# Chunked attention with a gated MLP: a list of moves behind the planner reorders two stretches of the late products

## The chip, the cores and the metric

The kernel runs on one core of a Trainium2 chip. The metric is the device time of one launch in microseconds (us). Three runs of the kernel before took 373.38, 374.20 and 375.71 us, median 374.2.

The engines are PE (TensorE, matrix products; PEld is its weight load), DVE (VectorE), ACT (ScalarE), POOL (GpSimd) and SP (SyncE, which here only issues transfers).

## The reference

The reference computes a chunked attention and feeds its result into a gated MLP whose gate mixes positions:

```python
x = attn_out.transpose(0, 2, 1, 3).reshape(B, S, H * D)   # B=4, S=768, 512 wide
h = np.maximum(x @ w_in, 0.0)                             # 512 -> 1024
u, v = h[..., :512], h[..., 512:]
v_n = (v - mean(v)) / np.sqrt(var(v) + 1e-06)
v_s = np.einsum('ts,bsd->btd', w_spatial, v_n) + b_spatial[None, :, None]
out = (u * v_s) @ w_out
```

Every chunk of 32 positions attends to itself, 16 positions to its left, 8 to its right and 8 memory slots.

## The kernel before

The first part, up to about 218 us, interleaves the attention with the product with w_in. Its results, u and the normalized v, are written to scratch in device memory (`u_far`, `vn_far`) and read back later (`ug`, `vr`).

The second part is the subject here. For each of the four batches b there are two products: the spatial one (`spatial(b)`, v_n with w_spatial) and the w_out one (`ffn_o(b)`). Each is written as seven smaller products p1 to p7 of half-size blocks (`product`, seven in place of eight), whose left operands are quarters of the input or sums of quarters. In fp32 accuracy each operand is split in a high and a low half, and three matmuls replace one: high·high, low·high, high·low.

A small product goes through the engines in this way:

- `total` (L670, DVE, 128x768): sums or differences of quarters, s1 to s4, in `sm` tiles.
- `left` (L684 on ACT casts the high half, L687 on DVE subtracts for the low half, 128x768): the split operand in an `op` tile.
- `blocks` (L707, PE): 9 matmuls of 128x384 a block for the spatial product, two blocks a small product; 6 matmuls of 128x256 a block for w_out, three blocks a small product. The first matmul of a block reads the high half only, the second reads the low half.
- `done`: an accumulator in a `y` bank of PSUM runs on from small product to small product. Before p6 may add to the bank that p1 filled, ACT copies p1's value out (`take`, L747 for spatial, L812 for w_out). DVE adds results of PSUM (`join`, L753 and L818), adds the bias (L772) and multiplies u by the gate for one quarter (L791). POOL adds a bias step (L767) and multiplies the other quarters (L761).

Beside the first spatial product, two splits of w_out run too (`right_hand` and `split`): sums on POOL (L919), casts on ACT (L890), low halves on DVE (L894). The last pieces of the first part overlap it as well: the norm of the last v tile (L597, DVE, between a `pow` on POOL, L593, and a store to `vn_far`), and four blocks of u, whose relu on ACT (L619) writes a `uo` tile that a store takes to `u_far`. There are two `uo` buffers, so a relu waits until the store of the relu two before it has landed.

All operations are recorded in a list with an engine, an estimated duration, dependences and a rank (`Plan.op`). `Plan.order` simulates them with these estimates and gives one order for the whole program; `emit` issues them in that order. Each engine executes its own in that order and waits on semaphores; SP issues the transfers (L284) in that order too, each as soon as its own wait is over, so that a store whose data are late holds up all transfers behind it. Negative numbers in the order are idle matmuls at the start that keep PE busy.

Of the kernel before, what the change touches and what calls it, by code (L numbers as in the profile page):

```python
# [18 lines left out]
CH = 32  # L19
SLOT = 40  # L20
LEFT = 16
FIRST = ('a', 'b', 'w0', 'v0', 'w1', 'w2', 'w3', 'q1', 'v1', 'w4', 'v2', 'w5', 'w6', 'w7')
RANKS = (34.7, 9.5, 12.7, 26.3, 36.3, 2.9, 37.5, 38.2)
LOWS = ('POOL', 'DVE', 'DVE', 'DVE', 'POOL', 'DVE', 'DVE', 'POOL')
# [4 lines left out]
class Plan:  # L29
# [121 lines left out]
        return none  # L151

    def emit(self):
        for n in self.order():
            if n < 0:
                self.idle(-n)
            else:
                self.ops[n][2]()


@with_exitstack
def tile_chunked_attention_gmlp(
# [106 lines left out]
    def src(t, offset, ap):  # L269
        return bass.AP(tensor=t.tensor, offset=offset, ap=ap)  # L270
# [20 lines left out]
    def load(dst, src_, w, rank, r=(), eng="SP", slow=1.0, us=0.45, seq=False, drag=1.0, of=None):  # L291
        e = {"SP": nc.sync, "ACT": nc.scalar, "POOL": nc.gpsimd}[eng]
        n = 4
        for s in src_.shape:
            n *= s
        mb = n / 1e6 * slow
        n = op(eng, us, lambda: transfer(e, dst() if callable(dst) else dst, src_, mb, of), r=r, w=w, rank=rank, mb=mb,
               after=line.get(eng) if seq else None, drag=drag)
        if seq:
            line[eng] = n  # L300
# [10 lines left out]
    def spot(name, g, shape):  # L311
        if (name, g) not in t_:
            alloc(name, g, shape, F32)
        return t_[name, g]

    def load_qk(g, units=(0, 1), seq=True):
# [3 lines left out]
        nk = 2 * UT + CH  # L320
        lo = LEFT if c0 == 0 else 0
        hi = nk - LEFT if c0 + 2 * UC == NC else nk
        q0, q1 = units[0] * UT, units[-1] * UT + UT
# [5 lines left out]
        load(lambda: spot("k", g, [P, T, nk])[:, :, k0:k1],  # L329
             src(k, off - LEFT + k0, [[S, P], [P * S, T], [1, k1 - k0]]), w=[ks + (u,)], rank=10.0 * i, slow=1.15, seq=seq)  # L330

# [55 lines left out]
    def spread_mem(i, eng, rank):  # L387
        b, o = i // UB, (i % NV) * UC
        for r in range(2):
            rows = slice(r * D + CH, r * D + SLOT)  # L390

            def spread(rows=rows, r=r):
                to, of = vmain[rows, :, o:o + UC], memv[rows, b].unsqueeze(2).broadcast_to([M, T, UC, D])
                ins = {"DVE": nc.vector, "POOL": nc.gpsimd}[eng].tensor_copy(to, of)  # L394
                made.setdefault(("vmem", i % NV), []).append(ins.ins.name)
            op(eng, 1.1 if eng == "POOL" else 1.25, spread, r=[("memv", r)], w=[("vmem", i % NV, r)], rank=rank)
# [65 lines left out]
    def softmax(i, rank):  # L462
        c0 = (i % UB) * UC

        def top():
            s = t_["sx", i][:, :, 0]
            if c0 == 0:
                nc.vector.memset(s[0:CH, :, :, 0:LEFT], NEG)
            if c0 + UC == NC:
# [497 lines left out]
    for j in range(NV):  # L967
        spread_mem(j, "DVE" if j < 1 else "POOL", 1.0 + 10 * j)
    for x in FIRST:
        if x[0] == "w":  # L970
# [105 lines left out]
```

## Time and profile before

| quantity | value |
|---|---|
| runs, median (lowest to highest) | 374.2 us (373.38 to 375.71) |
| time of the profiled execution | 373.39 us |
| span of its trace | 371.6 us |
| PE busy | 356.2 us, 96% of the span |
| DVE, ACT, POOL busy | 294.7, 186.9, 157.1 us |
| granted PE clock | 1.00 of full speed |

The span runs from the program's first instruction to its last; 1.8 us of the profiled time lie around it. A busy PE says that matmuls are in flight. The two stretches of the change lie, in the trace of before, at about 206 to 262 us and at about 328 to 372 us.

### The profile page before, as it was taken

How to read it: one execution, taken by the hardware profiler on the slowest of the kernel's cores; microseconds unless marked ns; L12 is line 12 of the kernel's file. 1: busy time of each engine (PE TensorE's matmuls, PEld its weight loads, DVE VectorE, ACT ScalarE, POOL GpSimd, SP SyncE). 2: the span in 40 equal slices, each digit the busy share in tenths (PEclk: the TensorE clock that was granted, in tenths of full speed). 3: DMA queues.
4: the chain of work that ended last, by engine and by line, in shares of the span. 5: the costliest groups of instructions: out<-in, count | busy, mean ns of one | idle time of the engine just before them, and what ended most of it. 6: DMA issues, size and time to landing. Idle time of an engine off the chain costs nothing. (4 is left out here: it accounts for less than half of the span.)

```text
span 371.6 us, 11928 instructions
## 1 busy us (share of the span) xinstructions
PE 356.2 (96%) x5026; PEld 328.6 (88%) x5026; DVE 294.7 (79%) x480; ACT 186.9 (50%) x334; POOL 157.1 (42%) x154
## 2 busy tenths in 40 slices
PE   2899999999999999999999999999999999999995
PEld 2787888988889889889888899989999999999895
DVE  3799968669669499584797689999979896998894
ACT  3577553655555445544483445347434733744451
POOL 6254733366376057720024367851246025216400
PEclk9999999999999999999999999999999999999999
DMA  8998977885895894968743538204830572230015
GB/s 209 291 246 242 233 223 244 260 249 164 251 241 179 217 276 136 266 159 272 222 168 101 215 132 308 94 1 155 228 129 2 196 227 88 85 130 0 0 44 170
DMA packets 47557, 65.52 MB, mean 176 GB/s; under 512 B 4496, under 2 KB 38928, under 8 KB 47504
## 3 DMA queue, kind: packets, MB, share of 16 engines
q1 hardware_dynamic: 46848, 64.44, 58.1%
q8 instruction: 39, 0.64, 0.8%
q10 hardware_dynamic: 656, 0.33, 0.3%
q14 instruction: 14, 0.11, 0.1%
HBM read 45.88 MB, written 18.87 MB: 174 GB/s over the span
## 5 line engine op out<-in xcount | busy, mean ns | idle before, releaser
L707 PE MATMUL y<-wsp,op 128*128 128x384 f32 x288 | 52.4, 337 | 0.0
L761 POOL TENSOR_TENSOR ug<-st,ug 128x384 f32<-128x384 f32 x24 | 34.5, 1453 | 40.1 <-DVE st L753 35.6
L707 PEld LDWEIGHTS y<-wsp,op 128*128 128x128 f32 x288 | 49.9, 188 | 0.4 <-ACT st L747 0.3
L557 PE MATMUL f<-x,win_h 128*128 128x384 f32 x128 | 46.0, 359 | 0.2 <-issue 0.2
L559 PE MATMUL f<-x,win_h 128*128 128x384 f32 x128 | 43.2, 338 | 0.0
L558 PE MATMUL f<-x,win_l 128*128 128x384 f32 x128 | 43.2, 337 | 0.0
L557 PE MATMUL f<-win_h,x 128*128 128x512 f32 x96 | 41.1, 428 | 0.0
L707 PE MATMUL f<-wsp,op 128*128 128x384 f32 x216 | 39.7, 337 | 0.0
L687 DVE TENSOR_TENSOR op<-sm,op 128x768 fp32r<-128x768 f32 x32 | 36.6, 1144 | 2.0 <-ACT op L684 1.8
L558 PE MATMUL f<-win_h,x 128*128 128x512 f32 x96 | 37.9, 395 | 0.1
L707 PEld LDWEIGHTS f<-wsp,op 128*128 128x128 f32 x216 | 37.5, 188 | 0.3 <-DVE st L753 0.3
L559 PE MATMUL f<-win_l,x 128*128 128x512 f32 x96 | 37.7, 393 | 0.0
L707 PE MATMUL y<-wout,op 128*128 128x256 f32 x288 | 36.0, 281 | 0.9 <-DVE op L687 0.8
L455 DVE TENSOR_TENSOR xs<-sx,rec 128x512 f32<-128x512 f32 x24 | 16.6, 690 | 24.6 <-PE sx L415 24.4
L707 PEld LDWEIGHTS y<-wout,op 128*128 128x128 f32 x288 | 34.6, 188 | 1.6 <-DVE op L687 1.5
L593 POOL TENSOR_TENSOR rstd<-ve,mhalf 128x1 f32<-128x1 f32 x24 | 14.5, 604 | 49.0 <-DVE ve L589 47.1
L684 ACT CAST op<-sm 128x768 fp32r<-128x768 f32 x32 | 26.4, 836 | 16.5 <-DVE sm L670 16.4
L767 POOL TENSOR_TENSOR st<-st,bias 128x384 f32<-128x384 f32 x14 | 17.9, 1286 | 38.3 <-ACT st L747 28.7
L415 PEld LDWEIGHTS sx<-kmain,q 64*32 64x32 f32 x1536 | 17.3, 109 | 14.3 <-issue 12.9
L581 ACT ACTIVATE st<-f 128x512 f32<-128x512 f32 x24 | 14.4, 599 | 28.7 <-PE f L559 28.2
L415 PE MATMUL sx<-kmain,q 64*32 64x64 f32 x1536 | 21.3, 230 | 7.4 <-ACT kmain L400 6.8
L394 POOL COPY vmain<-memv 8x1024 f32<-8x1024 f32 x22 | 23.9, 1090 | 9.9 <-PE sx L415 7.7
(86 smaller groups left out, 780.9 us busy)
## 6 DMA issues: line engine op xcount, KB each, us to landing
vmain<-in_v_dram SPq DMA_DIRECT2D x48, 128.0 KB
u_far<-uo SPq DMA_DIRECT2D x32, 192.0 KB
vn_far<-st SPq DMA_DIRECT2D x24, 256.0 KB
vr<-vn_far SPq DMA_DIRECT2D x8, 768.0 KB
ug<-u_far SPq DMA_DIRECT2D x16, 384.0 KB
q<-in_q_dram SPq DMA_DIRECT2D x11, 512.0 KB
vmain<-in_v_dram SPq DMA_DIRECT2D x47, 96.0 KB
out_dram<-ot SPq DMA_DIRECT2D x33, 128.0 KB
```

The lines of the kernel that those rows point to most:

```text
L394: ins = {"DVE": nc.vector, "POOL": nc.gpsimd}[eng].tensor_copy(to, of)
L415: ins = nc.tensor.matmul(o, w_, m, start=True, stop=True, skip_group_check=True)
L455: nc.vector.tensor_tensor(xs.rearrange("p t r d -> p r t d"), t_["sx", i][:, :, 1], rec.rearrange("p t r -> p r t").unsqueeze(3).broadcast ...
L557: nc.tensor.matmul(o, lh, rh, start=(j == 0), stop=False)
L558: nc.tensor.matmul(o, ll, rh, start=False, stop=False)
L559: nc.tensor.matmul(o, lh, rl, start=False, stop=(j == len(pairs) - 1))
L593: nc.gpsimd.tensor_tensor(a, t_["ve", i], mhalf, op=ALU.pow)
L684: nc.scalar.copy(half(0), of())
L687: nc.vector.tensor_tensor(half(1), of(), half(0).bitcast(F32), op=ALU.subtract)
L707: nc.tensor.matmul(o, x, y, start=first and m == 1, stop=m == 3 * chunks, skip_group_check=True)
L761: nc.gpsimd.tensor_tensor(g, t_[st(x)], g, op=ALU.mult)
L767: {"DVE": nc.vector, "POOL": nc.gpsimd}[eng].tensor_tensor(a, a, bias[:, 1], op=ALU.add)
```

## The change

A table `MOVES` of 119 pairs is added. `emit` takes the planner's order, and for each pair (n, m) takes operation n out and puts it right behind operation m. The idle matmuls of the start are now a second table, and stand where they stood. Two lines of the table:

```diff
+MOVES = (
+    (1035, 934), (1027, 975), (1036, 941), (1028, 948), (1037, 1028), (1038, 1037), (963, 951), (964, 950),
...
+    (1507, 1506), (1479, 1507), (1509, 1479), (1502, 1498), (1523, 1502), (1499, 1505),
+)
+IDLES = ((87, 5), (92, 4), (95, 2), (104, 29), (132, 1))
...
     def emit(self):
-        for n in self.order():
-            if n < 0:
-                self.idle(-n)
-            else:
-                self.ops[n][2]()
+        order = [n for n in self.order() if n >= 0]
+        for n, m in MOVES:
+            order.remove(n)
+            order.insert(order.index(m) + 1, n)
+        idles = dict(IDLES)
+        for n in order:
+            self.ops[n][2]()
+            if n in idles:
+                self.idle(idles[n])
```

No operation is added, removed or resized. The planner's order has 1560 operations; the two stretches that change are places 961 to 1190 and 1422 to 1514 in it. Lines of the changed kernel stand 22 further down (L597 becomes L619).

The first place is DVE at the end of the first part, where the last v tile is normalized. `sm` tiles are the sums s1, s2 of the first spatial product, `op` tiles its split operands, `st_3848` (now `st_3850`) the last v tile. Before:

```order
L597 TENSOR_SCALAR st_3824<-st_3824,mvar_3831,rstd_3841 128x512
L585 BN_STATS stats_3857<-st_3848 128x6
L587 BN_AGGR mvar_3859<-stats_3857 128x2
L589 TENSOR_TENSOR ve_3861<-mvar_3859,eps_103 128x1
L687 TENSOR_TENSOR op_3855<-vr_3798,op_3855 128x768
L597 TENSOR_SCALAR st_3848<-st_3848,mvar_3859,rstd_3874 128x512
L670 TENSOR_TENSOR sm_3888<-vr_3798,vr_3809 128x768
L687 TENSOR_TENSOR op_3883<-vr_3809,op_3883 128x768
L670 TENSOR_TENSOR sm_3908<-sm_3888,vr_3798 128x768
L687 TENSOR_TENSOR op_3917<-sm_3908,op_3917 128x768
L670 TENSOR_TENSOR sm_3908<-vr_3809,sm_3908 128x768
L687 TENSOR_TENSOR op_3928<-sm_3888,op_3928 128x768
```

And with the change:

```order
L619 TENSOR_SCALAR st_3824<-st_3824,mvar_3831,rstd_3841 128x512
L692 TENSOR_TENSOR sm_3848<-vr_3798,vr_3809 128x768
L607 BN_STATS stats_3861<-st_3850 128x6
L609 BN_AGGR mvar_3863<-stats_3861 128x2
L611 TENSOR_TENSOR ve_3865<-mvar_3863,eps_103 128x1
L692 TENSOR_TENSOR sm_3867<-sm_3848,vr_3798 128x768
L709 TENSOR_TENSOR op_3859<-vr_3809,op_3859 128x768
L709 TENSOR_TENSOR op_3876<-sm_3867,op_3876 128x768
L709 TENSOR_TENSOR op_3857<-vr_3798,op_3857 128x768
L709 TENSOR_TENSOR op_3915<-sm_3848,op_3915 128x768
L619 TENSOR_SCALAR st_3850<-st_3850,mvar_3863,rstd_3888 128x512
```

Two sums and three more low halves now stand ahead of the last norm, which had only one low half between it and its statistics.

The second place is ACT right after that. `uo` tiles are the last relus of u, `y_3935` and `y_3969` (now `y_3950` and `y_3971`) the two banks that p1 fills; their copies into `st` tiles are the takes that p6 waits for. Before:

```order
L619 ACTIVATE uo_3922<-f_3894 128x384
L684 CAST op_3928<-sm_3888 128x768
L619 ACTIVATE uo_3945<-f_3913 128x384
L890 CAST wout_3958<-big_3358 128x256
L890 CAST wout_3958<-big_3373 128x2x256
L890 CAST wout_3958<-big_3459 128x256
L890 CAST wout_3958<-big_3495 128x2x256
L747 COPY st_3988<-y_3935 128x384
L684 CAST op_4002<-sm_3986 128x768
L747 COPY st_4009<-y_3969 128x384
```

And with the change:

```order
L641 ACTIVATE uo_3923<-f_3880 128x384
L912 CAST wout_3943<-big_3358 128x256
L912 CAST wout_3943<-big_3373 128x2x256
L641 ACTIVATE uo_3946<-f_3905 128x384
L641 ACTIVATE uo_3960<-f_3884 128x384
L769 COPY st_3986<-y_3950 128x384
L706 CAST op_3990<-sm_3984 128x768
L912 CAST wout_3943<-big_3459 128x256
L769 COPY st_4011<-y_3971 128x384
```

The last relu now stands right ahead of the first take, and one cast has moved in between the two takes. On PE, p6 now starts with the bank `y_3971`, whose take is the second of the two.

The third place is DVE at the end of the last spatial product. `ug_5127` is the quarter that DVE gates itself, `op_5355` (now `op_5346`) the operand of p1 of the last w_out product, `op_5359` (now `op_5348`) that of p2 of the w_out product before it, which PE runs right behind p1. Before:

```order
L791 TENSOR_TENSOR ug_5127<-y_5015,ug_5127 128x384
L670 TENSOR_TENSOR sm_5357<-ug_5127,ug_4755 128x768
L753 TENSOR_TENSOR st_5265<-f_5270,st_5265 128x384
L687 TENSOR_TENSOR op_5355<-ug_4829,op_5355 128x768
L670 TENSOR_TENSOR sm_5373<-sm_5357,ug_4829 128x768
L753 TENSOR_TENSOR st_5281<-f_5287,st_5281 128x384
L687 TENSOR_TENSOR op_5359<-ug_4751,op_5359 128x768
L687 TENSOR_TENSOR op_5399<-sm_5373,op_5399 128x768
```

And with the change:

```order
L813 TENSOR_TENSOR ug_5127<-y_5015,ug_5127 128x384
L709 TENSOR_TENSOR op_5346<-ug_4829,op_5346 128x768
L692 TENSOR_TENSOR sm_5369<-ug_5127,ug_4755 128x768
L709 TENSOR_TENSOR op_5348<-ug_4751,op_5348 128x768
L692 TENSOR_TENSOR sm_5372<-sm_5369,ug_4829 128x768
L775 TENSOR_TENSOR st_5265<-f_5279,st_5265 128x384
L775 TENSOR_TENSOR st_5289<-f_5308,st_5289 128x384
L709 TENSOR_TENSOR op_5401<-sm_5372,op_5401 128x768
```

The low half for p2 now stands third behind the gate instead of sixth; the second sum and both joins come after it.

## Rows read from the trace of the kernel before

**Rows 1.** The page, busy time of PE with its share and instructions.

```profile
PE 356.2 (96%) x5026; PEld 328.6 (88%) x5026; DVE 294.7 (79%) x480; ACT 186.9 (50%) x334; POOL 157.1 (42%) x154
```

**Rows 2.** Chain of waits, in order of time: start, length, what.

```profile
291.40 4.20 PE y L707 x36
...
306.05 6.24 PE y L707 x36
```

**Rows 3.** Busy time by stretch: length, PE's busy time (matmuls), clock, DMA share, GB/s.

```profile
218.20:254.60 36.40, 35.50 (x217) 1.00 0.38 125
254.60:346.57 91.97, 91.97 (x629) 1.00 0.38 123
346.57:367.90 21.33, 20.66 (x163) 1.00 0.22 75
```

**Rows 4.** Timeline of PE: start, length, work, and idle time before it.

```profile
224.44 1.72 PE L707 MATMUL y<-wsp,op 128*128 128x384 f32 x9
...
246.85 0.28 PE L707 MATMUL y<-wout,op 128*128 128x256 f32 x1
247.97 4.36 PE L707 MATMUL y<-wout,op 128*128 128x256 f32 x35 [0.83 <-DVE op L687]
...
351.97 0.28 PE L707 MATMUL f<-wout,op 128*128 128x256 f32 x1
352.90 2.25 PE L707 MATMUL f<-wout,op 128*128 128x256 f32 x17 [0.65 <-DVE op L687]
```

**Rows 5.** Timeline of DVE round the last norms of v.

```profile
213.24 1.07 DVE L597 TENSOR_SCALAR st<-st,mvar,rstd 128x512 f32<-128x512 f32 x1 [0.44 <-POOL rstd L593]
...
215.76 1.50 DVE L687 TENSOR_TENSOR op<-vr,op 128x768 fp32r<-128x768 f32 x1
```

**Rows 6.** Busy time of DVE from one norm's end to the next's.

```profile
210.28:214.31 4.03, 3.07 (x6) 1.00 0.30 114
```

**Rows 7.** Timeline of SP's queue: issue time, length of the issue, transfer.

```profile
148.49 0.34 SPq L284 DMA_DIRECT2D u_far<-uo  x1
...
214.33 0.32 SPq L284 DMA_DIRECT2D vn_far<-st  x1
214.80 1.19 SPq L284 DMA_DIRECT2D u_far<-uo  x1
```

**Rows 8.** Busy by stretch after those two stores; the last two figures are the DMA's.

```profile
216.50:217.00 0.50, 0.50 (x5) 0.50 (x4) 0.50 (x1) 0.00 (x0) 0.50 (x1) 1.00 0.97 367
217.00:217.50 0.50, 0.50 (x4) 0.50 (x4) 0.50 (x2) 0.00 (x0) 0.50 (x1) 1.00 0.08 25
```

**Rows 9.** Timeline of ACT: a relu that waited for its buffer, and the second place.

```profile
152.64 0.49 ACT L619 ACTIVATE uo<-f 128x384 f32<-128x384 f32 x1 [0.22 <-DMA u_far<-uo]
...
221.06 1.86 ACT L890 CAST wout<-big 128x256 fp32r<-128x256 f32 x4
223.15 0.48 ACT L747 COPY st<-y 128x384 f32<-128x384 f32 x1 [0.23 <-DVE y L772]
224.06 0.83 ACT L684 CAST op<-sm 128x768 fp32r<-128x768 f32 x1 [0.43 <-DVE sm L670]
224.80 0.47 ACT L747 COPY st<-y 128x384 f32<-128x384 f32 x1
```

**Rows 10.** Timeline of DVE behind the last gate.

```profile
346.77 0.56 DVE L791 TENSOR_TENSOR ug<-y,ug 128x384 f32<-128x384 f32 x1 [0.93 <-PE y L707]
347.44 0.96 DVE L670 TENSOR_TENSOR sm<-ug 128x768 f32<-128x768 f32 x1
...
349.74 1.77 DVE L670 TENSOR_TENSOR sm<-sm,ug 128x768 f32<-128x768 f32 x1
...
351.90 0.94 DVE L687 TENSOR_TENSOR op<-ug,op 128x768 fp32r<-128x768 f32 x1
```

**Rows 11.** Timeline of DVE and of POOL at the same moment.

```profile
239.28 1.55 DVE L894 TENSOR_TENSOR wout<-st,wout 128x512 fp32r<-128x512 f32 x1
...
239.27 1.00 POOL L767 TENSOR_TENSOR st<-st,bias 128x384 f32<-128x384 f32 x1
```

13 rows, old and new, of the table MOVES are left out of this document.

## The prediction

> **What bounds the kernel now.** I read the page first. PE is busy for 96% of the span [rows 1], so a reordering can win only where PE stands still, or lose where it is made to. The chain of waits gives PE's cadence: 36 matmuls of 384 columns take 6.24 us and 36 of 256 columns 4.20 us [rows 2], so 0.1733 and 0.1167 us each.
>
> With that cadence the busy times by stretch say how much PE loses [rows 3]. From 218.20, where the spatial products begin, to 254.60 PE does 217 matmuls, 162 of the wide kind and 55 of the narrow: 28.08 + 6.42 = 34.50 us of work in 36.40 us, a **loss of 1.9 us**. Between the two stretches, from 254.60 to 346.57, it is busy without a break. From 346.57 to its end there are 18 wide and 144 narrow ones (one of the 163 began earlier): 3.12 + 16.80 us, and 0.16 us for the last one's drain, 20.1 us in 21.33, a **loss of 1.2 us**. All that this change could win by itself is therefore 3.1 us, 0.8% of the time. The granted clock is 1.00 in all three rows, across the waits too, so a matmul costs the same before and behind a wait.
>
> Then the timeline of PE shows who is waited for [rows 4]. At 246.85 the first matmul of p1 of the first w_out product starts, and the second, which needs the low half, follows only at 247.97: 1.0 us more than the cadence, and DVE L687 ended it. The rest of the first loss, 0.9 us, lies in smaller pieces. At 351.97 and 352.90 the same shows for p2 of batch 2's w_out product: 0.8 us. So in both stretches PE waits for low halves on DVE, and the question is whether the new order brings them sooner and what it makes late instead.
>
> **What DVE's operations cost.** A 128x768 operation takes 0.96 us alone and 1.77 us when POOL works beside it [rows 10]; in the first stretch, beside the w_out sums on POOL, a low half took 1.50 us [rows 5]. Which of the two goes first when they start together is settled by hundredths: at 239.27 POOL began 0.01 us ahead, ran its own 1.00 us, and DVE's operation took 1.55 [rows 11]. Each such meeting is worth some 0.8 us to DVE. I take the free price where no POOL work is due and 1.50 in the first stretch.
>
> **First stretch, the part that loses.** The last norm of v (L597) ended at 214.31 [rows 5]. From the norm before it to that moment DVE was busy for 3.07 of 4.03 us, 0.96 idle [rows 6]. The new order puts two sums (2 x 0.96) and three more low halves (3 x 1.50) ahead of this norm and lets the one low half that was there already fall beside POOL's sums (0.54 more), but fills the idle 0.96: 214.31 + 1.92 + 4.50 + 0.54 - 0.96 = **220.3 us**.
>
> Who waits for that norm? SP, first. Its store to vn_far was issued at once, at 214.33, and the next u_far store came right behind it, at 214.80 [rows 7]. SP keeps its order, so the vn_far store now goes at 220.3 and that u_far store at 220.8, though its data are ready earlier. In the trace the traffic of the same pair ran until between 217.0 and 217.5: a DMA share of 0.97 in the half microsecond before 217.0 and of 0.08 in the one after [rows 8], thus 2.2 to 2.7 us after the issue. With the middle, 2.45, it lands at 223.2.
>
> ACT is next. The last relu of u needs that store's buffer, and in the new order it stands ahead of the take of p1's first bank, a cast, a w_out cast and the take of p1's second bank. By rows these are 0.49, 0.48, 0.83, 0.47 (a quarter of four casts in 1.86) and 0.47 us [rows 9], 2.74 in sum, less 0.09 at each of four hand-overs, as 224.06 + 0.83 against 224.80 shows: 2.4 us. The second bank is thus copied out at 225.6. PE now starts p6 with just this bank and is there at 224.44, as before [rows 4], if nothing ahead of it on PE is late: p1's own low half moves behind two others and is ready two operations before that norm, at about 220.3 - 1.1 - 1.5 = 217.7, ahead of PE's 218.4. So **PE waits some 1.2 us at a place where it did not wait at all**, and about 0.1 more to get going.
>
> **First stretch, the part that gains.** The wait at 246.85 was for the low half of p1 of w_out. One w_out low half (1.55 us, the row's own price beside POOL [rows 11]) and one join (0.55, close to the gate's 0.56 [rows 10]) now stand behind it instead of ahead: 2.1 us sooner against a wait of 1.0. DVE also gets ahead by PE's new wait, since in this time it mostly works on inputs that are there already. The 0.9 us in smaller pieces should go the same way; I leave 0.1 for them. So the loss goes from 1.9 to 1.2 + 0.1 + 0.1 = 1.4 us: **0.5 us won**. Its bounds: if the store's landing does not hold up ACT at all, 1.8 us won; if it takes the 4.15 us of the third rival, 1.2 us lost.
>
> **Second stretch.** DVE's gate ends at 347.33, and the low half for p2 at 351.90 + 0.94 = 352.84 [rows 10], 5.5 us later; PE asks for it with p2's second matmul, at 351.97 + 0.12 = 352.09 [rows 4], 4.8 us behind the gate. The new order has only p1's low half and a sum ahead of it: 3 x 0.96 = 2.9 us behind the gate. The wait of 0.8 us goes, with 1.9 us to spare.
>
> Late next is the low half of s2, which PE needs after three blocks of p1 and two of p2. It stands behind a sum (0.96), two joins (2 x 0.55) and itself (0.96, or 1.77 beside POOL's gate): 5.6 to 6.4 us behind the gate, after 0.3 us for hand-overs. PE asks for it when p1's start, 2.4 us behind the gate by the cadence, is followed by five blocks of 0.70 and one matmul: 6.0 us. So from no wait to 0.4. With the small waits behind it I leave 0.4 of the 1.2 us (bounds 0 and 1.2): **0.8 us won**. The end of the program keeps its order: the last three blocks, their joins and the split stores.
>
> **Sum.** 0.5 + 0.8 = 1.3 us. The profiled execution took 373.4 us, so it would take 372.1. It was at the lower end of the runs shown; their median, 374.2, is 0.8 above it. A median of the changed kernel should therefore fall between 372.1 and 372.9; I name **372.5 us**.
>
> **The first rival, chance 0.15: the store lands in time.** If the relu is not held up, because the norm meets less of POOL or the store lands in little over a microsecond, PE meets no new wait, and 1.8 + 0.8 = 2.6 us are won: 370.8 us by the profiled execution. For it: the walk along DVE took 1.50 us for each low half, and POOL might be elsewhere. Against it: POOL's w_out sums are not moved away, and even at the free price for all four low halves the norm ends at 218.0, some 3.7 us later than before.
>
> **The second rival, chance 0.10: the waits only move.** DVE and POOL have the same work in both stretches, and what was moved behind comes due some microseconds later; PE would lose the same 3.1 us elsewhere, and the time stays at 373.4 (374.2 in the median). For it: DVE is nearly full in the first stretch. Against it: PE is unbroken for 92 us from 254.60 on [rows 3], so what is put off has room there.
>
> **The third rival, chance 0.15: slower, by the store's landing.** One u relu in the trace shows directly how long a store of this kind can hold its buffer: issued at 148.49 [rows 7], and the relu that waited for it began at 152.64 [rows 9], 4.15 us later, with loads of v around it. In the new order ug loads follow the store within a microsecond. At 4.15 instead of 2.45 us PE waits 2.9 us instead of 1.2, the first stretch loses 1.2 us, the second wins 0.8, and the time is 373.8. The point from which it decides is a landing 3.8 us after the issue, where gain and loss cancel; each microsecond beyond is a microsecond, so 375 us at 5.4.
>
> The Trainium skill bears on this rival: DMA: Bandwidth & Descriptors, in its anatomy of one DMA (written for transfers of another issuing path), says that a transfer's semaphore moves only once the last byte is confirmed as landed, and that this makes most of a fixed cost of about 2.0 us. By that rule the wait would end later than the traffic that I took as its end, up to 4.7 us after the issue, and the sum would be 374.3; no run here shows the moment of the semaphore itself.
>
> **Chances and range.** The forecast has 0.60. It spans 371.5 to 373.4, with the 0.8 us between profiled execution and median in it. 370.4 to 374.9 takes in the first rival against the profiled execution, the second against the median, and most of the third: 8 in 10 or a little more. One per cent, 3.7 us, is about what a measurement of this kernel can tell from no change. To be faster by that, PE would have to lose all its waits and the runs fall well besides: 0.04. To be slower by it, a wait of more than 5 us would have to arise: 0.05. Within 1%: 0.91.
>
> **What would show it.** Right: in the changed profile the last norm (now L619) ends near 220, the u_far store is issued right behind the vn_far store at 220 to 221, PE stands still before its third small product near 224.4 for a microsecond or more, ended by ACT's copy out of y, and no wait for DVE is left at p1 of w_out near 247 or at p2 near 352. Wrong: no idle time of PE near 224.4 (first rival), idle time of PE for DVE's low halves at new places that adds up to 3 us (second), or an ACT relu that starts after 225 (third).

## The result, and the profile after

| quantity | before | changed kernel |
|---|---|---|
| median of the runs | 374.95 us (6 runs) | 370.98 us (6 runs, 369.22 to 372.67) |
| ratio | | 0.989, 95% interval 0.9856 to 0.9925 |
| time of the profiled execution | 373.39 us | 369.22 us |
| span of its trace | 371.6 us | 367.4 us |
| PE from its first spatial block to its last matmul | 149.7 us | 146.4 us |

The forecast was 372.5 us with a range of 370.4 to 374.9. The time lies in the range, 1.5 us below the number, because the range took in the first rival; the likeliest case did not happen: the new wait stayed away.

The last row of the table is the measure of all that follows. Runs of one kernel spread over several microseconds, and much of that comes from the first part: over the eleven traces of this study the first spatial block starts anywhere between 217.33 (the changed kernel) and 225.28 us, although the order ahead of it is the same but for the last few microseconds. From that block on the granted clock is 1.00 in all eleven traces, also in the two that were taken in slow runs (the second one of the changed kernel and the one of the two key moves). So from there the traces can be compared to one or two tenths: the changed kernel took 146.4 and 146.5 us in two of them, with starts 6 us apart. There the change wins 149.7 - 146.4 = **3.3 us**, 0.9%; the rest of the 4.2 us between the two profiled executions lies ahead of the stretches.

The stretches of the changed kernel, in the columns of [rows 3]:

```profile
217.33:253.00 35.67, 35.67 (x228) 1.00 0.44 157
253.00:346.71 93.71, 93.71 (x639) 1.00 0.35 115
346.71:363.90 17.19, 17.00 (x145) 1.00 0.27 93
```

PE is busy without a break from the first block to the end (the last row's 0.19 us lie behind its last matmul, at 363.71). All waits of [rows 4] are gone. The places where they stood, in PE's timeline after:

```profile
223.58 3.29 PE L729 MATMUL y<-wsp,op 128*128 128x384 f32 x18
...
245.42 2.27 PE L729 MATMUL y<-wout,op 128*128 128x256 f32 x18
247.52 0.86 PE L729 MATMUL f<-wout,op 128*128 128x256 f32 x6
...
348.82 1.56 PE L729 MATMUL f<-wout,op 128*128 128x256 f32 x12
350.22 0.86 PE L729 MATMUL y<-wout,op 128*128 128x256 f32 x6
```

No row carries an idle time: not p6 at 223.58, where the forecast put one of 1.2 us, not p1 of w_out at 245.42, and not p2 at 348.82. The rows also show the new order on PE in the w_out products: behind p1 (in `y`, at 245.42) a block of p5 (in `f`, at 247.52) now runs before p6, which stood right behind p1 before.

The chain that the forecast followed is all there. DVE in the changed kernel, where [rows 5] had the norm at 213.24:

```profile
212.08 0.95 DVE L709 TENSOR_TENSOR op<-vr,op 128x768 fp32r<-128x768 f32 x1
213.07 1.50 DVE L709 TENSOR_TENSOR op<-sm,op 128x768 fp32r<-128x768 f32 x1
214.50 1.61 DVE L709 TENSOR_TENSOR op<-vr,op 128x768 fp32r<-128x768 f32 x1
216.03 1.50 DVE L709 TENSOR_TENSOR op<-sm,op 128x768 fp32r<-128x768 f32 x1
217.45 1.08 DVE L619 TENSOR_SCALAR st<-st,mvar,rstd 128x512 f32<-128x512 f32 x1
```

Then SP, whose u_far store waits behind the vn_far store (against [rows 7]), and ACT, whose last relu waits for that u_far store before it can take p1's banks (against [rows 9]):

```profile
218.55 0.32 SPq L306 DMA_DIRECT2D vn_far<-st  x1
...
218.96 0.38 SPq L306 DMA_DIRECT2D u_far<-uo  x1
...
221.11 0.49 ACT L641 ACTIVATE uo<-f 128x384 f32<-128x384 f32 x1 [2.13 <-DMA u_far<-uo]
221.50 0.48 ACT L769 COPY st<-y 128x384 f32<-128x384 f32 x1
...
222.91 0.49 ACT L769 COPY st<-y 128x384 f32<-128x384 f32 x1
```

This is the margin: the second bank is copied out at 222.91 + 0.49 = 223.40, and PE is ready for it at 223.58. The forecast's wait stayed away by **0.18 us**.

### The profile page after: what moved, and what is told of

Same layout as the page of the kernel before. It is cut to its first block, busy times and chain, and to the rows that moved or that the text cites. A ratio compares the mean times of both kernels' runs of the same rounds, so it can differ in the third digit from the quotient of the medians.

```text
span 367.4 us, 11909 instructions
## 1 busy us (share of the span) xinstructions
PE 354.0 (96%) x5026; PEld 328.2 (89%) x5026; DVE 288.8 (79%) x480; ACT 186.2 (51%) x334; POOL 155.8 (42%) x154
## 4 chain that ended last, share of the span: by engine, by line
PE 87%; DMA 5%; DVE 4%; ACT 2%; issue 1%; SPq 0%; ACTq 0%
PE y L729 23%; PE f L729 16%; PE f L579 12%; PE f L580 11%; PE f L581 11%; PE sx L437 9%; DMA k<-in_k_dram 3%; PE pt L525 3%; PE xt L541 3%; DMA vmain<-in_v_dram 2%; DVE st L893 1%; DVE st L892 1%; DVE p L498 1%; DVE mx L494 1%; DVE ve L611 0%
## 5 line engine op out<-in xcount | busy, mean ns | idle before, releaser
L709 DVE TENSOR_TENSOR op<-sm,op 128x768 fp32r<-128x768 f32 x32 | 34.7, 1087 | 4.0 <-ACT op L706 3.6
```

Source lines behind the costliest of these rows:

```text
L709: nc.vector.tensor_tensor(half(1), of(), half(0).bitcast(F32), op=ALU.subtract)
```

## The experiments

All are read by the measure above: PE's time from its first spatial block to its last matmul, in one trace of each kernel. The three that move the norm, the one that moves a store on SP and the one with PE's order taken back were each executed once; for the others the ratio of the runs is given too.

**Each stretch alone.** The list cut after its 79th pair, and the 40 pairs behind it alone:

```diff
 first stretch alone:
...
+    (1160, 1155), (1161, 1160), (1151, 1173), (1157, 1151), (1142, 1157), (1143, 1142), (1175, 1185),
+    (1098, 1198), (1095, 1098),
+)
 second stretch alone:
+MOVES = (
+    (1443, 1419), (1446, 1443), (1435, 1446), (1465, 1435), (1421, 1465), (1447, 1421), (1459, 1429),
...
```

> Only the first 79 pairs of the list, those of the first stretch. Measure: time of PE from the start of its first spatial block to the end of its last matmul, which leaves the first part's scatter out: 149.7 us before (218.20 to 367.88), 146.4 in the changed kernel (217.33 to 363.71). Theory (the two stretches are independent, each wins what PE lost in it): 147.5 to 147.6, 2.1 us won; the wait of 0.8 us for the low half of p2 is still there in the second stretch. Rival (waits only move, the whole is won by the two lists together): the first list alone leaves the second stretch worse than before, 148.5 or more. In runs 371.5 to 372.5 us against some 374.5 before.

> Only the last 40 pairs, those of the second stretch. Same measure. Theory (independent): 148.5 us, 1.2 us won; the wait at p1 of the first w_out product stays at 0.8 to 1.0 us. Rival (what the second list wins depends on the first one's order): under 0.5 us won, 149.2 or more. In runs 373 to 373.8 us.

Measured: 147.8 us with the first stretch alone (1.9 won) and 148.4 with the second alone (1.3 won), together 3.2 of 3.3. In runs the ratios are 0.9954 (0.9913 to 0.9995) and 0.9921 (0.988 to 0.9961), too wide to rank them; 1.3 us of 374.9 would be 0.9965, just above the second interval, so the runs show at least what the measure shows. PE and ACT with the first list alone, at p6, and PE at p2 of the second stretch:

```profile
225.81 2.94 PE L726 MATMUL f<-wsp,op 128*128 128x384 f32 x16
228.72 2.52 PE L726 MATMUL y<-wsp,op 128*128 128x384 f32 x13
...
228.17 0.49 ACT L766 COPY st<-y 128x384 f32<-128x384 f32 x1
...
354.24 0.28 PE L726 MATMUL f<-wout,op 128*128 128x256 f32 x1
355.17 2.25 PE L726 MATMUL f<-wout,op 128*128 128x256 f32 x17 [0.65 <-DVE op L706]
```

And with the second list alone, at p1 of the first w_out product:

```profile
247.15 0.28 PE L720 MATMUL y<-wout,op 128*128 128x256 f32 x1
248.10 4.12 PE L720 MATMUL y<-wout,op 128*128 128x256 f32 x33 [0.68 <-DVE op L700]
```

Each list removes the waits of its own stretch and leaves those of the other as they were. In the first list's run p6 started late by 228.72 - 225.81 - 16 x 0.1733 = 0.14 us, and the matmul behind it by another 0.1: there the margin of 0.18 us was just missed. Up to this place the order is that of the changed kernel, but the last norm ended 1.45 us behind the first spatial block instead of 1.20, and the second bank was copied out at 228.17 + 0.49 = 228.66, after PE was due at 228.58. So with one and the same order the wait comes in one trace and stays away in another.

**The two key moves alone.** The forecast gave the wins to two low halves that come sooner. So these two, and nothing else, were moved in the planner's order:

```diff
-MOVES = (
-    (1035, 934), (1027, 975), (1036, 941), (1028, 948), (1037, 1028), (1038, 1037), (963, 951), (964, 950),
...
+MOVES = (
+    (1100, 1107), (1483, 1475),
+)
```

> The planner's order with two pairs alone: the low half of p1 of the first w_out product right behind the sum s1, and the low half of p2 of batch 2's w_out product right behind the low half of p1 of batch 3's. Theory (two late low halves make most of the loss): the waits of 1.0 and 0.8 us go and at most 0.5 us comes back behind them, at the low halves of s2, which are not moved: 148.0 to 148.4 us by the same measure, 1.3 to 1.7 won of 3.3. Rival (DVE is full in both stretches, so a wait removed by one move comes back at the next low half): 149.2 us or more.

Measured: **150.4 us, 0.7 more than before the change** (runs: ratio 1.0026, 0.9984 to 1.0067, which is no change clear of noise, and no win). The theory fell. PE at the first w_out product, DVE and ACT there:

```profile
253.93 2.26 PE L715 MATMUL y<-wout,op 128*128 128x256 f32 x18
257.36 2.37 PE L715 MATMUL y<-wout,op 128*128 128x256 f32 x18 [1.17 <-ACT ot L820]
...
251.88 1.76 DVE L695 TENSOR_TENSOR op<-ug,op 128x768 fp32r<-128x768 f32 x1
...
256.20 0.83 ACT L692 CAST op<-sm 128x768 fp32r<-128x768 f32 x1
256.93 0.93 ACT L820 COPY ot<-y 128x256 f32<-128x256 f32 x3
```

The wait in p1 is gone: its 18 matmuls run in one piece. But p6 follows at 257.36 where 253.93 + 18 x 0.1167 = 256.03 was due, 1.3 us late, and it is not a low half that it waits for: ACT's take of p1's bank stands behind a cast. The moved low half met POOL (1.76 us) and pushed DVE's bias additions and the second sum, and with them ACT's takes and casts, behind it. In the second stretch the same run shows 0.6 us at p6 for a low half and 0.4 for ACT. The waits moved, as the forecast's second rival had it.

**PE's order alone taken back.** Then something else in the list must win. DVE, ACT, POOL and SP keep the changed kernel's order, PE gets the planner's:

```diff
-        order = [n for n in self.order() if n >= 0]
+        plan = [n for n in self.order() if n >= 0]
+        order = list(plan)
...
+        rows = {e: [n for n in (plan if e == "PE" else order) if self.ops[n][0] == e] for e in ENGINES}
+        place, done, merged = {n: i for i, n in enumerate(order)}, set(), []
+        while len(merged) < len(order):
+            n = min((q[0] for q in rows.values() if q and self.ops[q[0]][3] <= done), key=place.get)
+            rows[self.ops[n][0]].pop(0)
+            done.add(n)
+            merged.append(n)
+        order = merged
```

> The changed kernel's order on DVE, ACT, POOL and SP, but PE keeps the planner's order of blocks, as before the change. Measure: PE from its first spatial block to its last matmul, 149.7 us before, 146.4 in the changed kernel. Theory (the moved low halves, sums and takes are ready early enough for either order of blocks): 146.4 to 147.0 us. Rival (the run with two moves alone came to 150.4 us, because PE, which went from p1 straight to p6, then waited 1.2 us for ACT's takes; so the moves on PE, which put a block of p5 between them, carry part of the gain): PE waits for takes or low halves at p6 and behind, 147.5 us or more.

Measured: 150.8 us, all of the gain lost and 1.1 more. The waits of PE in this run, by what it waited for, total, times, longest:

```profile
PE y L738 <- ACT st L778: 0.9, 1, 0.9
PE y L738 <- ACT st L843: 0.6, 1, 0.6
PE f L738 <- DVE op L718: 0.4, 1, 0.4
PE f L738 <- DVE st L849: 0.3, 1, 0.3
```

Two of them are takes. One, in PE's timeline:

```profile
340.31 1.72 PE L738 MATMUL y<-wsp,op 128*128 128x384 f32 x9
342.99 2.35 PE L738 MATMUL y<-wsp,op 128*128 128x384 f32 x12 [0.95 <-ACT st L778]
```

1.1 us more than the cadence. The two waits of [rows 4] are not among the four; others have come in their place. So the new orders on the other engines are worth nothing without the blocks of PE that were moved with them: these give the takes, the joins and the low halves the time that they need. The opposite, PE's new order with the planner's order elsewhere, is not shown: with all its moves the engines would wait for each other in a circle in the second stretch, and in the first stretch alone, where they would not, it was not run.

**The chain that nearly bound.** Four kernels ask whether the forecast's chain (norm, SP's queue, relu, take, p6) is real and where it binds. The first is the changed kernel unaltered; three move the norm:

```diff
 earlier:  +    (942, 941), (943, 1028),
 late:     +    (1068, 1046),
 later:    +    (1068, 1046), (1049, 1068),
```

> The changed kernel once more, unaltered. In its first trace ACT had copied the second bank of p1 out at 223.40 and PE was ready for it at 223.58, 0.18 us to spare. Theory (the order of the engines is fixed, so the margin repeats within a tenth or two): 146.3 to 146.6 us by the same measure and no wait of PE before p6 of more than 0.1 us. Rival (the margin is luck, because the landing of a store varies by half a microsecond or more): a wait of 0.3 us or more before p6, 146.7 or more.

> The changed kernel with the last norm of v three low halves earlier on DVE, right behind the low half of p2; SP's order stays. Measure as before: PE from its first spatial block to its last matmul, 146.4 us in the changed kernel. Theory (the chain norm, store, relu, take had 0.18 us to spare, so it cost nothing): 146.4 us, within 0.1; the norm ends some 4 us sooner, the last relu and the takes no longer wait for a store. Rival (the low halves that now stand behind the norm come too late, since the low half of p1 had 1.4 us to spare and the norm takes 1.1 beside POOL): PE waits 0.2 to 0.7 us at p1, 146.6 to 147.1.

> The changed kernel with the sum s4 ahead of the last norm of v, so that the norm is one operation of 1.50 us later (less 0.08 of hand-over); nothing else moves. Theory (the chain of the forecast is there, norm to store on SP to relu to take to p6, with 0.18 us to spare): the norm ends 1.4 us later, PE waits 1.2 us before p6 for ACT's copy out of y, 147.6 us by the same measure. Rival (the chain has more slack than the trace shows, or the relu waits for something else): no wait before p6, 146.4 us.

> The changed kernel with the sums s4 and s3 ahead of the last norm: 1.42 + 0.87 = 2.3 us later. Theory: PE waits 2.1 us before p6, 148.5 us by the same measure, a microsecond for each microsecond. Rival (the wait does not grow with the delay, because another wait ends last): under 1.5 us, 147.9 or less.

Measured: 146.5, 146.4, 147.8 and 148.8 us; in the runs of the first 0.9922 (0.9881 to 0.9963). The unaltered kernel's ACT and PE:

```profile
225.11 0.38 SPq L306 DMA_DIRECT2D u_far<-uo  x1
...
227.26 0.49 ACT L641 ACTIVATE uo<-f 128x384 f32<-128x384 f32 x1 [2.12 <-DMA u_far<-uo]
...
229.06 0.49 ACT L769 COPY st<-y 128x384 f32<-128x384 f32 x1
...
229.72 3.28 PE L729 MATMUL y<-wsp,op 128*128 128x384 f32 x18
```

Its margin is 229.72 - 229.06 - 0.49 = 0.17 us, as in the first trace. With the norm later by one sum, SP, ACT and PE:

```profile
222.34 0.38 SPq L309 DMA_DIRECT2D u_far<-uo  x1
...
224.48 0.49 ACT L644 ACTIVATE uo<-f 128x384 f32<-128x384 f32 x1 [3.53 <-DMA u_far<-uo]
...
226.27 0.49 ACT L772 COPY st<-y 128x384 f32<-128x384 f32 x1
...
226.82 2.35 PE L732 MATMUL y<-wsp,op 128*128 128x384 f32 x12 [1.12 <-ACT st L772]
```

And PE with the norm later by two sums:

```profile
227.22 2.00 PE L732 MATMUL y<-wsp,op 128*128 128x384 f32 x10 [2.12 <-ACT st L772]
```

Against the cadence p6 comes 1.3 and 2.3 us late. With the norm earlier PE did not wait either, and the time stayed at 146.4: in the changed kernel the chain costs nothing. Counted from the first block, the norm ended 1.4 and 2.4 us later than in the changed kernel, so the wait is the delay less the margin, to a tenth. The wait that the forecast foretold exists, at the engine and the block that it named, and grows a microsecond for each one. In the two traces of the changed kernel it is only just not there.

**SP's order taken out of it.** The last one keeps the norm late by two sums and moves its vn_far store behind the two u_far stores:

```diff
+    (1068, 1046), (1049, 1068), (944, 962),
```

> As the kernel before in this list, with sums s4 and s3 ahead of the norm, but the vn_far store of this norm two places later on SP, behind the u_far stores of two relus; DVE, ACT and PE keep the order of that kernel. Theory (what the norm holds up is SP's queue, and through it the u_far store whose buffer the last relu needs): the u_far store is issued as soon as its relu is done, near 217, the last relu starts near 219, PE does not wait before p6, 146.4 us. Rival (the late norm holds up DVE's own work or the takes directly): the wait stays, 148.5 us.

Measured: 146.6 us. SP, ACT and PE:

```profile
218.31 0.32 SPq L309 DMA_DIRECT2D u_far<-uo  x1
...
219.76 0.94 ACT L644 ACTIVATE uo<-f 128x384 f32<-128x384 f32 x2
222.85 0.48 ACT L772 COPY st<-y 128x384 f32<-128x384 f32 x1 [2.15 <-DVE y L797]
...
224.28 0.48 ACT L772 COPY st<-y 128x384 f32<-128x384 f32 x1
...
224.83 3.37 PE L732 MATMUL y<-wsp,op 128*128 128x384 f32 x18
```

The store no longer waits, both relus run back to back at 219.76, and PE starts p6 without a wait, though the norm is as late as in the kernel that lost 2.3 us. So it was SP's queue that made the wait. But the rival is not all wrong: the first take now waits 2.15 us for a bias addition on DVE (L797), which stands behind the late norm, and the second bank is copied out at 224.28 + 0.48 = 224.76, 0.07 us before PE is there. A norm that came later still would hold up the takes through DVE too.

## Why the prediction was off, step by step

**What bounds the kernel, and the most that can be won:** right. 3.1 us were read from the stretches and 3.3 were won; most of the missing 0.2 are late starts just behind 254.60, in a row of 92 us that was taken as unbroken [rows 3].

**The new wait at p6:** wrong in size, right in place. In time behind the first spatial block, with the forecast's own numbers less 218.20 and the trace's less 217.33:

| step | forecast | changed kernel |
|---|---|---|
| last norm ends | 2.1 | 1.2 |
| u_far store issued | 2.6 | 1.6 |
| last relu starts | 5.0 | 3.8 |
| second bank copied out | 7.4 | 6.1 |
| PE ready for p6 | 6.2 | 6.25 |

The mis-sized term is the first: the norm ended 0.9 us sooner. Half of that is a low half that ran free of POOL (0.95 at 212.08; the four took 5.56 us where 6.0 were put in), the other half the 0.08 us by which seven of the ten DVE operations start before the one ahead of them ends (the other three start 0.03 after it), counted at ACT's hand-overs but not at DVE's. The landing gave 0.3 more: 2.15 us from issue to relu where 2.45 was taken as the middle of a window of DMA traffic, and ACT's chain 0.1. In all 1.3 us against a wait of 1.2. So the first rival came true in its outcome, at a chance of 0.15: PE met no new wait. Its condition did not: the relu was held up, by 2.13 us, and the store took 2.15 us, not little over one; of its reasons only the norm's meeting less of POOL is borne out, for one low half of four. What the forecast had wrong is the size of the chain, not its path. It should have set its 1.2 us against the error of a sum of a dozen terms, and shared the chance between the two more evenly; that the chain ended on the near side by 0.18 us is luck, as the trace with the first list alone shows.

**The third rival, a landing 4.15 us after the issue:** excluded here. The waiting relu began 2.15, 2.15, 2.14 and 2.13 us after the u_far store's issue in the changed kernel, its repetition and the two late ones, although loads of `ug` followed within a microsecond. The rule that the prediction took from the Trainium skill (DMA: Bandwidth & Descriptors, anatomy of one DMA: about 2.0 us of fixed cost, most of it the confirmation) was set on top of the end of the traffic; the 4.7 us that came of it were not seen. That section of the Trainium skill has the fixed cost cover setup and completion and adds only the bytes at 436 GB/s: an estimate by it for 197 kB is 2.0 + 0.45 = 2.45 us in all, 0.3 more than the 2.14 measured.

**The waits that go, first stretch:** right that both kinds go, incomplete in the reason. The forecast gave the gain to the low half alone. The run with the two key moves shows that this low half by itself turns PE's wait into one for a take on ACT, and the run with PE's planned order that without the reordered blocks nothing of the gain is left. The forecast had PE's new order in its sums, but gave it no share in the gain. Which of the moves on DVE, ACT and POOL are needed beside them stays open.

**Second stretch:** right that the 0.8 us wait goes. The remainder of 0.4 us at the low half of s2 did not come. It was put at 5.6 to 6.4 us behind the gate, depending on whether POOL's gate meets it, and took 5.4: from the gate's end at 343.80 + 0.56 = 344.36 to 348.79 + 0.96 = 349.75. DVE and POOL there:

```profile
343.80 0.56 DVE L813 TENSOR_TENSOR ug<-y,ug 128x384 f32<-128x384 f32 x1 [1.00 <-PE y L729]
...
348.79 0.96 DVE L709 TENSOR_TENSOR op<-sm,op 128x768 fp32r<-128x768 f32 x1
...
348.84 1.80 POOL L783 TENSOR_TENSOR ug<-st,ug 128x384 f32<-128x384 f32 x1 [4.86 <-DVE st L775]
```

PE asked for it 6.0 us behind the gate, as forecast (the second matmul of the block at 350.22). DVE was first by 0.05 us and paid 0.96; POOL paid 1.80 where the same operation takes 1.0 alone. It is [rows 11] with the sides changed, and hand-overs between DVE's operations gave the other 0.2 us.

**The sum:** 3.3 won instead of 1.3. Of the 2.0 us between, 1.4 are the wait at p6 with its restart and the remainder left beside it, 0.4 the remainder in the second stretch, 0.2 the restarts not counted. The measured medians differ by 4.0 us, in the second measurement the ratio 0.9922 makes it 2.9; 3.3 us is a ratio of 0.991 and lies in both intervals. **The second rival**, that the waits only move, was given 0.10 for the whole list and did not happen; it is what happened when two of its moves alone were applied, and when all but PE's were.

No version beat the changed kernel: PE has no wait left behind 217 us (by the cadence its 504 wide and 504 narrow matmuls and the drain make 146.3 us, and it took 146.4), and each part taken away or altered cost time or changed nothing.

## What to carry to other kernels

A wait of the bounding engine names only what was late last; when its row says "low half on DVE", ask what comes next on every engine that feeds that block, here ACT's copies out of the banks, before giving the gain to one operation. Here the reordering paid because the consumer's order was changed together with the producers': the producers' order without PE's cost 1.1 us, and PE's without theirs is not shown. And a forecast wait that is the small difference of two long chains is a coin toss: compare it with the error of the sum (here 1.3 us in a chain of a dozen terms), or check how far it is from binding by making its first link later on purpose.

## What the runs showed of the hardware

A 197 kB store from a `uo` tile gave its buffer back 2.13 to 2.15 us after its issue in six kernels (besides the four above, those with the first list alone and with PE's planned order, 2.14 each). In all six a vn_far store had gone out 0.4 us ahead of it. In the two kernels where none went so close ahead (the norm earlier, and SP's order changed), the relu started 1.89 and 1.90 us after the issue with no idle of ACT before it, so the buffer was back by then. In [rows 9] it took 4.15 us, where loads of v and q ran around it.

After each stop of PE the first matmul is followed by a gap some 0.11 us longer than the cadence (after all 23 late starts of 0.1 us or more in the seven traces that have any): in [rows 4] the 17 matmuls from 352.90 take 2.25 us, where 17 x 0.1167 and 0.16 for the drain make 2.14. The idle time in a row leaves out another 0.16 us, since it counts from the drain of the matmul before: 0.28 us after its start, where the cadence is 0.12. So a wait costs some 0.27 us more than its row says: at 247.97 the row has 0.83, and PE lost 1.00 against the cadence and 0.11 behind it.
